# Windowed attention and a rational-function FFN: from the framework's schedule to an order made by a list scheduler in the kernel source

## The chip, the cores and the metric

The kernel runs on one core of one Trainium2 chip. The metric is the device time of one execution in microseconds; the lower the better. Before the change, three runs took 1013.21, 1014.49 and 1015.51 us, so the median is 1014.49.

## The reference

Attention with 8 batches, 8 heads, 576 positions and 64 features per head. Each position sees itself and the 63 positions before it. The 4608 rows of 512 features that come out go through a feed-forward layer whose activation is a quotient of two polynomials.

```python
scores = scale * np.matmul(q, k.transpose(0, 1, 3, 2))
mask = (rel >= 0) & (rel < window)            # window = 64
scores = np.where(mask, scores, -1000000000.0)
attn = np.exp(scores - np.max(scores, axis=-1, keepdims=True))
attn = attn / (np.sum(attn, axis=-1, keepdims=True) + 1e-09)
x = np.matmul(attn, v)                        # then 4608 x 512
h = x @ w_in                                  # w_in 512 x 2048
P = a[0] + a[1] * h + a[2] * h**2 + a[3] * h**3
Q = 1.0 + np.abs(b[0]) * np.abs(h) + np.abs(b[1]) * h**2
out = (P / (Q + 1e-6)) @ w_out                # w_out 2048 x 512
```

The weights arrive as 64-bit floating-point numbers and are decoded on the chip.

## The kernel before

**Tiling.** The 4608 tokens are 12 chunks of 384. A chunk has an attention part of four *units* (two heads each), and an FFN part of 16 *steps*, one for each 128 of the 2048 hidden features. There are 192 steps and 48 units. The order of the steps is: first half of chunk 0, first half of chunk 1, second half of chunk 1, second half of chunk 0, then chunks 2 to 11 whole. So the weights of the first eight steps are used twice before those of the second half are needed, at step 16.

**A weight block** (`decode`, L110, 32 of them: 16 of `w_in`, 16 of `w_out`): a load of 512 KB, an ACT operation (L124), one on POOL (L127), two on DVE (L128, L129), one on ACT (L132, the high part) and one on DVE (L133, the low part). High and low parts stay in SBUF for the whole run.

**A unit** (L153 to L249): loads of q, k and v; 12 rows of score matmuls on PE into `ps_s` (L200); for chunks 1 and 2 the mask is added by two further matmuls (L193), for the others by two operations on DVE (L211); a maximum (L214, or L207 with L208); six exponentials on ACT (L221, L218); sums and reciprocals (L223, L224); the normalisation (L225), which is on DVE for chunk 0 and on POOL for the rest; transposes on PE into the same single `ps_s` buffer (L232) and a copy of them on ACT (L234); value products on PE (L243); the result split in a high and a low part, `xh` on ACT (L248) and `xl` on DVE (L249).

**A step** has two products on PE with a gate between them. `ffn1` (L253): 12 matmuls into one of two `h` buffers (L258); then the gate, with five operations on ACT (L265 to L267, L273, L274), one on POOL (L270) and six on DVE (L268, L269, L275 to L278). DVE's last one writes `gl`, the low half of the gate; `gh` is the high half. L269 is the last one to read `h`. `ffn2` (L288): nine matmuls (L298) that add the step's share to three accumulators `o`. I write H(s) and O(s) for the two products of step s.

**Half results.** When the first half of chunk 0 ends, its three accumulators are copied to a constant SBUF tile `part` (L305), and added back on DVE (L310) at the end of the second half.

**What sets the order.** The program text issues loads, units, H(s) and O(s - 3) from a table `todo`, with blocks and units placed at fixed steps (L322 to L347). The tile framework then schedules the instructions again by its own timeline simulation (`schedule_with_timeline_sim=True`, L403), so the order on each engine isn't that of the text. Each engine works through its own queue in order, and so does the queue of DMAs on SP.

**Buffers** that matter here: three stages for loaded weights (`w_st`), two `w_c`, two v tiles, two sets of gate temporaries (`tmp`), four pairs `gh`, `gl` (`gp`), two `h`, one `ps_s`, one `ps_x`.

Of the kernel before, what the change touches and what calls it, by code (L numbers as in the profile page):

```python
# [22 lines left out]
W_AT = 0, 1, 2, 3  # L23
WLEAD = len(W_AT)
NEG = -1.0e30
PEM = 1, 2
QADD = 1.0 + 1e-6


@with_exitstack  # L30
def swa_rational_ffn(ctx: ExitStack, tc: tile.TileContext, qT, kT, v, w_in, w_out, a, b, out):
# [20 lines left out]
    gp = ctx.enter_context(tc.tile_pool(name="gp", bufs=LAG + 1))  # L52
# [57 lines left out]
    def decode(src, hi, lo):  # L110

        w = stage.tile([P, 512, 2], U32, name="w_st", bufs=3)
        if len(src.shape) == 3:
            nc.sync.dma_start(out=w.rearrange("p (c n) two -> p c (n two)", c=src.shape[1]), in_=src)
        else:
            nc.sync.dma_start(out=w.rearrange("p n two -> p (n two)"), in_=src)
        low, high = w[:, :, 0], w[:, :, 1]
        c = stage.tile([P, 512], U32, name="w_c")
        cf = c.bitcast(F32)

        highf = w.bitcast(F32)[:, :, 1]
        nc.scalar.activation(cf, highf, AF.Copy, scale=2.0 ** -111)  # L124


        nc.gpsimd.tensor_scalar(out=highf, in0=highf, scalar1=0.0, scalar2=None, op0=ALU.mult)  # L127
        nc.vector.scalar_tensor_tensor(out=c, in0=c, scalar=3, in1=high, op0=ALU.logical_shift_left, op1=ALU.bitwise_or)  # L128
        nc.vector.scalar_tensor_tensor(out=c, in0=low, scalar=29, in1=c, op0=ALU.logical_shift_right, op1=ALU.bitwise_or)  # L129
        if len(hi.shape) == 3:  # L130
            cf = cf.rearrange("p (c n) -> p c n", c=hi.shape[1])
        nc.scalar.activation(hi, cf, AF.Copy, scale=2.0 ** -8)  # L132
        nc.vector.scalar_tensor_tensor(out=lo, in0=cf, scalar=2.0 ** -8, in1=hi.bitcast(F32), op0=ALU.mult, op1=ALU.subtract)  # L133

    def load_w_in(i):
        sl = slice(i * P, (i + 1) * P)
        decode(w_in[i], wi_h[:, :, sl], wi_l[:, :, sl])

    def load_w_out(i):
        decode(w_out_v[:, i, :], wo_h[:, i, :], wo_l[:, i, :])  # L140
# [12 lines left out]
    def unit_load(c, hp):  # L153
        q = kv.tile([P, TC, WIN], F32, name="q")
        kt = kv.tile([P, TC + 1, WIN], F32, name="kt")
        vt = kv.tile([P, TC, P], F32, name="vt")
        kw, vw, first = [], [], None
        j = kb = vb = 0
        for bi, t0, n in segments(c):
            nc.sync.dma_start(out=q[:, j:j + n, :].rearrange("p t s -> p (t s)"),  # L160
                              in_=qT[bi, hp, :, t0 * WIN:(t0 + n) * WIN])
# [16 lines left out]
        m0 = None if first is None else MASKS[first]
        live[c, hp] = dict(q=q, kt=kt, vt=vt, kw=kw, vw=vw, m0=m0)
# [108 lines left out]
    def ffn2(s):  # L288
# [3 lines left out]
        if first:  # L292
            acc[c] = [ps_o.tile([P, DO], F32, name=f"o{t}") for t in range(NTS)]
# [115 lines left out]
```

## Time and profile before

| | |
|---|---|
| median of 3 runs | 1014.49 us (1013.21 to 1015.51) |
| span of the profiled execution | 1014.7 us |
| PE busy | 954.8 us (94%) |
| DVE busy | 825.9 us (81%) |
| ACT busy | 725.1 us (71%) |
| POOL busy | 324.9 us (32%) |
| mean granted clock of TensorE | 0.971 |
| read and written in HBM | 53.48 and 9.44 MB |

The profile lists the span, from the first to the last instruction; what may lie around it has no row. Durations below are of this one execution. Busy shares are means over the whole run, so the table alone doesn't say what bounds which stage. "Idle before" in a row is time in which the engine had nothing to do ahead of that group, with what ended it. Records of one engine overlap a little, since an instruction's end is pipelined with the start of the next: start to start is shorter than the duration shown.

### The profile page before, as it was taken

Reading aid. Unit: us, or ns where it says so; the run is one execution under the profiler, and the core shown is the slowest. Engines: PE = TensorE matmul, PEld = TensorE weight load, DVE = VectorE, ACT = ScalarE, POOL = GpSimd, SP = SyncE. Lnnn points to the kernel's source line nnn. Section 1 sums busy time; section 2 is a strip of 40 time slices with the busy share of each in tenths; the row PEclk is TensorE's granted clock in tenths of the full one; section 3 lists DMA queues with packets and bytes.
Section 4 is the critical chain, followed back from the end, with each engine's and each line's share of the span. In section 5 each row is a group of like instructions: output and inputs, shape, how many; then the busy total and the mean of one; then the engine's idle time right before and its main releaser. Section 6 shows DMA issues by size and latency. Waiting matters only on the chain.

```text
span 1014.7 us, 18277 instructions
## 1 busy us (share of the span) xinstructions
PE 954.8 (94%) x6640; PEld 844.8 (83%) x6640; DVE 825.9 (81%) x1539; ACT 725.1 (71%) x1735; POOL 324.9 (32%) x283
## 2 busy tenths in 40 slices
PE   3688578999999999999999999999999999999997
PEld 2576367989898888898888888888988988988996
DVE  7899788878888788788788787787787888787885
ACT  5777666667676777877777777777777777777664
POOL 4566544223332222223223223223223223222221
PEclk9679789999999999999999999999999999999999
DMA  7634630021211211210211211110121111100000
GB/s 239 221 110 138 207 98 16 1 77 29 90 31 31 83 42 34 88 37 29 76 46 31 67 58 34 64 61 29 61 61 31 62 63 35 64 17 1 32 1 31
DMA packets 37817, 64.09 MB, mean 63 GB/s; under 512 B 4448, under 2 KB 24928, under 8 KB 37728
## 3 DMA queue, kind: packets, MB, share of 16 engines
q1 hardware_dynamic: 37728, 62.93, 19.4%
q8 instruction: 52, 0.85, 0.4%
q14 instruction: 37, 0.30, 0.1%
HBM read 53.48 MB, written 9.44 MB: 62 GB/s over the span
## 4 chain that ended last, share of the span: by engine, by line
PE 84%; DVE 10%; ACT 3%; issue 2%; POOL 1%; DMA 1%; SPq 0%; POOLq 0%; DVEq 0%
PE h L258 38%; PE o L298 37%; PE ps_x L243 3%; PE ps_s L200 3%; PE ps_s L232 3%; DVE w_c L128 2%; POOL w_st L127 1%; DVE w_c L129 1%; DVE wo_l L133 1%; DVE num L277 1%; DVE u L276 1%; DVE wi_l L133 1%; DVE gh L275 1%; DMA w_st<-w_in 1%; ACT w_c L124 0%
## 5 line engine op out<-in xcount | busy, mean ns | idle before, releaser
L270 POOL TENSOR_TENSOR u<-u,ah 128x384 f32<-128x384 f32 x192 | 198.2, 1033 | 383.3 <-ACT u L267 343.7
L258 PE MATMUL h<-xl,wi_h 128*128 128x384 f32 x768 | 267.5, 348 | 20.3 <-DVE num L269 18.6
L258 PE MATMUL h<-xh,wi_h 128*128 128x384 f32 x768 | 262.7, 342 | 0.0
L258 PE MATMUL h<-xh,wi_l 128*128 128x384 f32 x768 | 262.5, 342 | 0.0
L298 PE MATMUL o<-wo_h,gl 128*128 128x512 f32 x576 | 233.5, 405 | 7.2 <-DVE gl L278 7.2
L298 PE MATMUL o<-wo_h,gh 128*128 128x512 f32 x576 | 228.3, 396 | 0.0
L298 PE MATMUL o<-wo_l,gh 128*128 128x512 f32 x576 | 227.0, 394 | 0.0
L268 DVE TENSOR_TENSOR num<-num,h 128x384 f32<-128x384 f32 x192 | 106.2, 554 | 111.9 <-ACT num L266 111.5
L265 ACT ACTIVATE ah<-h 128x384 f32<-128x384 f32 x192 | 94.5, 492 | 124.1 <-PE h L258 84.9
L258 PEld LDWEIGHTS h<-xl,wi_h 128*128 128x128 f32 x768 | 147.3, 192 | 27.8 <-DVE num L269 20.7
L258 PEld LDWEIGHTS h<-xh,wi_h 128*128 128x128 f32 x768 | 147.4, 192 | 4.8
L225 POOL TENSOR_TENSOR sm<-sm,rs 128x768 f32<-128x768 f32 x44 | 68.4, 1555 | 253.2 <-DVE rs L224 250.5
L258 PEld LDWEIGHTS h<-xh,wi_l 128*128 128x128 f32 x768 | 147.0, 191 | 0.6 <-issue 0.2
L275 DVE SCALAR_TENSOR_TENSOR gh<-num,a_sb,ah 128x384 fp32r<-128x384 f32 x192 | 119.3, 633 | 28.4 <-ACT ah L274 28.3
L298 PEld LDWEIGHTS o<-wo_h,gl 128*128 128x128 f32 x576 | 109.0, 189 | 33.7 <-DVE gl L278 8.8
L267 ACT ACTIVATE u<-ah,b_sb 128x384 f32<-128x384 f32 x192 | 135.6, 707 | 0.0
L221 ACT ACTIVATE sm<-sm,nmx 128x128 f32<-128x128 f32 x240 | 93.3, 390 | 57.4 <-DVE nmx L214 57.4
L298 PEld LDWEIGHTS o<-wo_h,gh 128*128 128x128 f32 x576 | 109.3, 190 | 25.2
L266 ACT ACTIVATE num<-h,a_sb 128x384 f32<-128x384 f32 x192 | 128.3, 668 | 0.0
L298 PEld LDWEIGHTS o<-wo_l,gh 128*128 128x128 f32 x576 | 109.2, 190 | 18.5
L269 DVE SCALAR_TENSOR_TENSOR num<-num,a_sb,h 128x384 f32<-128x384 f32 x192 | 117.7, 614 | 6.1
L277 DVE SCALAR_TENSOR_TENSOR num<-num,a_sb,u 128x384 f32<-128x384 f32 x192 | 116.7, 622 | 0.4
(52 smaller groups left out, 1139.2 us busy)
## 6 DMA issues: line engine op xcount, KB each, us to landing
out<-ob SPq DMA_DIRECT2D x33, 256.0 KB, 2.5
w_st<-w_in SPq DMA_DIRECT2D x16, 512.0 KB, 3.7
w_st<-w_out SPq DMA_DIRECT2D x16, 512.0 KB, 4.2
q<-qT SPq DMA_DIRECT2D x32, 192.0 KB, 3.2
vt<-v SPq DMA_DIRECT2D x16, 384.0 KB, 3.1
vt<-v SPq DMA_DIRECT2D x16, 320.0 KB, 3.0
kt<-kT SPq DMA_DIRECT2D x16, 224.0 KB, 3.6
kt<-kT SPq DMA_DIRECT2D x16, 192.0 KB, 3.4
```

Source lines behind the costliest of these rows:

```text
L221: nc.scalar.activation(sm[:, j, :], sm[:, j, :], AF.Exp, bias=nmx[:, j:j + 1], accum_out=sums[:, j:j + 1])
L225: (nc.vector if c < 1 else nc.gpsimd).tensor_tensor(out=sm, in0=sm, in1=rs.unsqueeze(2).broadcast_to([P, NR, P]), op=ALU.mult)
L258: nc.tensor.matmul(h, w[:, cc, i * P:(i + 1) * P], x[c, cc], start=n == 0, stop=n == 3 * NCC - 1)
L265: nc.scalar.activation(ah, h, AF.Abs)
L266: nc.scalar.activation(num, h, AF.Identity, scale=a_sb[:, 3:4], bias=a_sb[:, 2:3])
L267: nc.scalar.activation(u, ah, AF.Identity, scale=b_sb[:, 1:2], bias=b_sb[:, 0:1])
L268: nc.vector.tensor_tensor(out=num, in0=num, in1=h, op=ALU.mult)
L269: nc.vector.scalar_tensor_tensor(out=num, in0=num, scalar=a_sb[:, 1:2], in1=h, op0=ALU.add, op1=ALU.mult)
L270: nc.gpsimd.tensor_tensor(out=u, in0=u, in1=ah, op=ALU.mult)
L275: nc.vector.scalar_tensor_tensor(out=gh, in0=num, scalar=a_sb[:, 0:1], in1=ah, op0=ALU.add, op1=ALU.mult)
L277: nc.vector.scalar_tensor_tensor(out=num, in0=num, scalar=a_sb[:, 0:1], in1=u, op0=ALU.add, op1=ALU.subtract)
L298: nc.tensor.matmul(acc[c][t], g[:, ts], w[:, i, :], start=first and n == 0, stop=last and n == 2)
```

## The change

The program text no longer issues work as it goes. Each piece is first described as an `Op`: its engine, a cost in microseconds, a rank (about the step at which it is wanted), what it comes after, and the buffers that it takes. `Plan.order` then builds a schedule: on each engine it looks for the operations that could start first, and among those within 0.02 us of the earliest takes the one of the lowest rank. It counts a hand-over of 0.035 us between engines, the overlap at an operation's end (`TAIL`), buffers that come free, one DMA bus, and half as much again for a DVE operation that runs beside POOL. The instructions are emitted in the order of the planned starts, in a section in which the framework leaves the order alone.

```diff
+class Plan:
+    LATENCY = 0.035
+    TAIL = {"PE": 0.16, "DVE": 0.083, "ACT": 0.105, "POOL": 0.0}
...
+    def order(self):
...
+            for e in ENGINES:
+                able = []
+                for op in ready[e]:
+                    if any(not slots[s.pool] for s in op.takes):
+                        continue
+                    t = max([free[e], op.ready] + [min(slots[s.pool]) for s in op.takes])
+                    able.append((t, op))
...
+                t0 = min(t for t, _ in able)
+                t, op = min(((t, op) for t, op in able if t <= t0 + 0.02), key=lambda x: (x[1].rank, x[0]))
+                if best is None or t < best[0]:
+                    best = t, op
...
+            if op.shares and free["POOL"] > t:
+                cost += 0.5 * min(cost, free["POOL"] - t)
...
+        return sorted(self.ops, key=lambda o: o.start)
...
-    gp = ctx.enter_context(tc.tile_pool(name="gp", bufs=LAG + 1))
+    gp = ctx.enter_context(tc.tile_pool(name="gp", bufs=3))
...
+    plan = Plan({"w_st": 3, "w_c": 2, "qk": 2, "vt": 1, "sm": 2, "pT": 1, "ps_s": 1, "ps_x": 1, "h": 2, "tmp": 2, "gp": 3,
+                 "o0": 1, "o1": 1, "o2": 1, "spill": 1})
...
+        o = plan.add("SP", 2.3, rank - 2, load, uses=[st])
+        o = plan.add("ACT", 0.68, rank, scale, [o], [st, sc])
+        o = plan.add("POOL", 1.75, rank, sign, [o], [st])
+        o = plan.add("DVE", 0.685, rank, put_sign, [o], [st, sc], True)
+        o = plan.add("DVE", 0.685, rank, put_low, [o], [st, sc], True)
+        o = plan.add("ACT", 0.635, rank, high, [o], [sc])
+        return plan.add("DVE", 0.685, rank, rest, [o], [sc], True)
...
+            vt = u["vt"] = kv.tile([P, TC, P], F32, name="vt", bufs=1)
...
-        (nc.vector if c < 1 else nc.gpsimd).tensor_tensor(out=sm, in0=sm, in1=rs.unsqueeze(2).broadcast_to([P, NR, P]), op=ALU.mult)
+            nc.gpsimd.tensor_tensor(out=sm, in0=sm, in1=u["rs"].unsqueeze(2).broadcast_to([P, NR, P]), op=ALU.mult)
...
+        f = f1[s] = plan.add("PE", 2.245, s, products, x_ready[c] + [tile_in[i], f1.get(s - 1)], [sh])
...
+            o = plan.add("PE", 0.855, s + LAG + 0.5 + 0.01 * t, lambda t=t: products(t),
+                         [gate_done[s], tile_out[i], f2.get((s - 1, t)), f2.get((s, t - 1))], [sg, so[t]])
...
-            part[c] = const.tile([P, NTS, DO], F32, name="part")
-            for t in range(NTS):
-                nc.scalar.copy(out=part[c][:, t, :], in_=o[t])
+                ob = e["ob"] = stage.tile([P, DO], F32, name="spill", bufs=1)
...
+                part[c, t] = tc.dram_tile([P, DO], F32, name=f"part{c}_{t}")
+                nc.sync.dma_start(out=part[c, t], in_=e["ob"])
...
+        tile_in[i] = plan_decode(w_in[i], wi_h[:, :, sl], wi_l[:, :, sl], need[i] - 1.5)
+        tile_out[i] = plan_decode(w_out_v[:, i, :], wo_h[:, i, :], wo_l[:, i, :], need[i] + LAG - 1.5)
...
+    load_coefficients()
+    with tc.manual_schedule():
+        for op in plan.order():
+            op.emit()
```

Beside the order, five things change. There is one v tile in place of two. There are three `gh`, `gl` pairs in place of four. The half results of chunk 0 go through one SBUF buffer (`spill`) to a tile in DRAM and are fetched into weight stages before they are added. The normalisation of chunk 0 moves from DVE to POOL. The two loads of coefficients stand ahead of all others. The steps, the units, their chunks and the arithmetic stay.

Three places in the order. The first is DVE after the low half of gate 7. Before, a long run of decode operations stands here (`w_c`, `wi_l`, `wo_l` are the decode's):

```order
L133 SCALAR_TENSOR_TENSOR wo_l<-w_c,wo_h 128x512
L129 SCALAR_TENSOR_TENSOR w_c<-w_st,w_c 128x512
L133 SCALAR_TENSOR_TENSOR wi_l<-w_c,wi_h 128x4x128
L128 SCALAR_TENSOR_TENSOR w_c<-w_c,w_st 128x512
L129 SCALAR_TENSOR_TENSOR w_c<-w_st,w_c 128x512
L128 SCALAR_TENSOR_TENSOR w_c<-w_c,w_st 128x512
L133 SCALAR_TENSOR_TENSOR wo_l<-w_c,wo_h 128x512
L129 SCALAR_TENSOR_TENSOR w_c<-w_st,w_c 128x512
L249 TENSOR_TENSOR xl_915<-ps_x,xh_914 128x384
```

Now, behind the same gate, operations of the gates alternate with those of the decode (L241, L246 and L257 are now the decode's three, L452 to L482 the gate's six):

```order
L469 SCALAR_TENSOR_TENSOR gh<-num,a_sb,ah 128x384
L241 SCALAR_TENSOR_TENSOR w_c<-w_c,w_st 128x512
L473 SCALAR_TENSOR_TENSOR u<-u,gh 128x384
L246 SCALAR_TENSOR_TENSOR w_c<-w_st,w_c 128x512
L477 SCALAR_TENSOR_TENSOR num<-num,a_sb,u 128x384
L452 TENSOR_TENSOR num<-num,h 128x384
L482 TENSOR_TENSOR gl<-num,ah 128x384
L257 SCALAR_TENSOR_TENSOR wo_l<-w_c,wo_h 128x512
```

What moved: when the low half of gate 12 is done, 31 blocks were decoded before and 18 are now; for gate 20 it is 32 and 26, for gate 23 it is 32 and 31, for gate 24 both have all 32.

The second is PE around O(23), the output products of step 23. Before, they follow value products, and a masked score group comes after them:

```order
L243 MATMUL ps_x<-pT,vt 64x64 x12
L298 MATMUL o_1267<-wo_h,gl 128x512
L298 MATMUL o_1267<-wo_l,gh 128x512
L298 MATMUL o_1267<-wo_h,gh 128x512
L298 MATMUL o_1268<-wo_h,gl 128x512
L298 MATMUL o_1268<-wo_l,gh 128x512
L298 MATMUL o_1268<-wo_h,gh 128x512
L298 MATMUL o_1269<-wo_h,gl 128x512
L298 MATMUL o_1269<-wo_l,gh 128x512
L298 MATMUL o_1269<-wo_h,gh 128x512
L193 MATMUL ps_s<-mask,ident_r 128x384 x2
```

Now H(26) and a score group (L335) stand ahead of them, and H(27) behind:

```order
L437 MATMUL h<-xh_0_503,wi_l 128x384
L335 MATMUL ps_s<-kt,q 64x128 x12
L520 MATMUL o_1346<-wo_h,gl 128x512
L520 MATMUL o_1346<-wo_l,gh 128x512
L520 MATMUL o_1346<-wo_h,gh 128x512
L520 MATMUL o_1381<-wo_h,gl 128x512
L520 MATMUL o_1381<-wo_l,gh 128x512
L520 MATMUL o_1381<-wo_h,gh 128x512
L520 MATMUL o_1439<-wo_h,gl 128x512
L520 MATMUL o_1439<-wo_l,gh 128x512
L520 MATMUL o_1439<-wo_h,gh 128x512
L437 MATMUL h<-xl_0_263,wi_h 128x384
```

What moved: by O(23) the new order has issued the score groups of units 11 and 12 and the transposes of unit 11, which stood behind it; the number of H and O groups issued is the same.

The third is PE in a late unit. Before, value products and the next unit's scores are adjacent:

```order
L258 MATMUL h<-xh_2288,wi_l 128x384
L243 MATMUL ps_x<-pT,vt 64x64 x12
L200 MATMUL ps_s<-kt,q 64x128 x12
L298 MATMUL o_2696<-wo_h,gl 128x512
L298 MATMUL o_2696<-wo_l,gh 128x512
```

Now transposes (L378) and value products (L388) stand two output groups apart, and the score group stands two steps ahead of the transposes:

```order
L378 MATMUL ps_s<-ident,sm 128x128 x6
L520 MATMUL o_2674<-wo_h,gl 128x512
L520 MATMUL o_2674<-wo_l,gh 128x512
L520 MATMUL o_2674<-wo_h,gh 128x512
L520 MATMUL o_2681<-wo_h,gl 128x512
L520 MATMUL o_2681<-wo_l,gh 128x512
L520 MATMUL o_2681<-wo_h,gh 128x512
L388 MATMUL ps_x<-pT,vt 64x64 x12
L520 MATMUL o_2708<-wo_h,gl 128x512
```

What moved: the unit's three groups lie in three places. Between them H(s) and O(s - 3) now alternate one by one, where before two H often stood together, then two O. At the very end H(191) has O(188) to O(191) behind it, where it had O(189) to O(191).

More of the change, by code (lines that the diff above doesn't have):

```diff
@@ L30, in swa_rational_ffn @@
+ENGINES = "PE", "DVE", "ACT", "POOL", "SP"
 @with_exitstack
@@ L108, in swa_rational_ffn @@
     w_out_v = w_out.rearrange("(fc p) e -> p fc e", p=P)
[L110 to L140, printed above, removed]
+    C0 = 2
+    HA = 8
+    NU = HP
+    phases = [(c, 0, HA) for c in range(C0)] + [(c, HA, NF) for c in reversed(range(C0))] + [(c, 0, NF) for c in range(C0, NCH)]
+    steps = [(c, i) for c, i0, i1 in phases for i in range(i0, i1)]
+    total = len(steps)
+    begin, at = {}, {}
+    for s, (c, i) in enumerate(steps):
+        begin.setdefault(c, s)
+        at[c, i] = s
@@ L289, in ffn2, with plan_out @@
+    acc, part, sent = {}, {}, {}
+    so = {}
+    f2 = {}
+    def plan_out(s):
         c, i = steps[s]
@@ L291, in ffn2 @@
         last = s == total - 1 or steps[s + 1][0] != c
+        d, sg = gs.pop(s)
         if first:
-            acc[c] = [ps_o.tile([P, DO], F32, name=f"o{t}") for t in range(NTS)]
-        gh, gl = gs.pop((c, i))
-        for t in range(NTS):
-            ts = slice(t * P, (t + 1) * P)
-            for n, (g, w) in enumerate(((gl, wo_h), (gh, wo_l), (gh, wo_h))):
-                nc.tensor.matmul(acc[c][t], g[:, ts], w[:, i, :], start=first and n == 0, stop=last and n == 2)
-        if not last:
-            return
@@ L365, in swa_rational_ffn @@
[L365 to L375 removed]
+            for t in range(NTS):
+                so[t] = Slot(f"o{t}")
+        spill = c < C0 - 1 and i < HA
+        merge = c < C0 - 1 and i >= HA
@@ new lines, in products, with fetch @@
+        def products(t):
+            if first:
+                acc[t] = ps_o.tile([P, DO], F32, name=f"o{t}")
+            ts = slice(t * P, (t + 1) * P)
+            for n, (g, w) in enumerate(((d["gl"], wo_h), (d["gh"], wo_l), (d["gh"], wo_h))):
+                nc.tensor.matmul(acc[t], g[:, ts], w[:, i, :], start=first and n == 0, stop=last and n == 2)
+        def fetch(t, e):
+            ob = e["ob"] = stage.tile([P, DO], F32, name="ob", tag="w_st", bufs=3)
+            nc.sync.dma_start(out=ob, in_=part[c, t])
@@ new lines, in swa_rational_ffn @@
+    for c, i0, i1 in phases:
+        if c not in seen:
+            before = begin[c] - prev
+            for k in range(NU):
+                order.append((c, k, -12 + k if c == 0 else before + (prev // NU) * k - AHEAD))
+            seen.append(c)
+        prev = i1 - i0
+    last_step = {}
+    for s, (c, i) in enumerate(steps):
+        last_step[c] = s
+    holder = {}
+    n = 0
+    s = 0
+    for c, k, rank in order:
+        if c >= C0 and k == 0:
+            old = max(x for x in range(c) if slot_of[x] == slot_of[c])
+            while s <= last_step[old]:
+                plan_gate(s)
+                s += 1
+            free_x[c] = [f1[last_step[old]]]
+        plan_unit(c, k, rank)
@@ L378 @@
+    while s < total:
+        plan_gate(s)
+        s += 1
+    for s in range(total):
+        plan_out(s)
+    load_coefficients()
+    with tc.manual_schedule():
+        for op in plan.order():
+            op.emit()
 _OUTS = [((4608, 512), 'float32')]
```

489 lines of the change are left out of this document (305 added, 184 removed).

## The prediction

> **What bounds the kernel now.** I read the page's busy slices first, then the same question by stage in a table of windows, then the operations of DVE in the early stage.
>
> ```profile
> PE   3688578999999999999999999999999999999997
> DVE  7899788878888788788788787787787888787885
> ...
> 5.40:163.00 157.60, 107.37 (x799) 89.82 (x800) 142.26 (x232) 108.82 (x277) 85.48 (x52) 0.83 0.49 157
> ...
> 300.00:900.00 600.00, 600.00 (x4301) 535.46 (x4301) 485.56 (x939) 449.19 (x1091) 172.76 (x157) 1.00 0.16 51
> ```
>
> In the slices (25.4 us each) PE is full from the seventh on. In the windows (length, then busy PE, PEld, DVE, ACT, POOL) PE is busy 600 of 600 us late, but 107.37 of 157.60 early, where DVE is busy 142.26: idle for only 15.3 us. So there are two stages. Late, PE is the bound and nothing that another engine saves is worth anything. Early, DVE is, and the longest waits of PE are for it:
>
> ```profile
> PE h L258 <- DVE num L269: 18.6, 7, 5.9
> ```
>
> Now what DVE did in those 157.6 us (by line: busy us, mean ns, idle before):
>
> ```profile
> L129 DVE SCALAR_TENSOR_TENSOR w_c<-w_st,w_c 128x512 uint32<-128x512 uint32 x32 | 26.0, 814 | 0.2
> L128 DVE SCALAR_TENSOR_TENSOR w_c<-w_c,w_st 128x512 uint32<-128x512 uint32 x32 | 25.0, 781 | 6.8 <-POOL w_st L127 6.6
> L133 DVE SCALAR_TENSOR_TENSOR wo_l<-w_c,wo_h 128x512 fp32r<-128x512 f32 x16 | 13.3, 833 | 0.4 <-ACT wo_h L132 0.4
> L133 DVE SCALAR_TENSOR_TENSOR wi_l<-w_c,wi_h 128x512 fp32r<-128x512 f32 x16 | 12.7, 791 | 1.9 <-ACT wi_h L132 1.9
> L275 DVE SCALAR_TENSOR_TENSOR gh<-num,a_sb,ah 128x384 fp32r<-128x384 f32 x13 | 10.6, 812 | 3.0 <-ACT ah L274 3.0
> L277 DVE SCALAR_TENSOR_TENSOR num<-num,a_sb,u 128x384 f32<-128x384 f32 x13 | 9.8, 756 | 0.1
> L276 DVE SCALAR_TENSOR_TENSOR u<-u,gh 128x384 f32<-128x384 f32 x13 | 9.1, 702 | 0.2
> L269 DVE SCALAR_TENSOR_TENSOR num<-num,a_sb,h 128x384 f32<-128x384 f32 x14 | 8.4, 602 | 0.0
> L268 DVE TENSOR_TENSOR num<-num,h 128x384 f32<-128x384 f32 x14 | 7.5, 543 | 0.0
> L278 DVE TENSOR_TENSOR gl<-num,ah 128x384 fp32r<-128x384 f32 x13 | 7.1, 547 | 0.0
> L207 DVE TENSOR_REDUCE nmx<-ps_s 128x6 f32<-128x768 f32 x6 | 5.7, 946 | 0.0
> L249 DVE TENSOR_TENSOR xl<-ps_x,xh 128x384 fp32r<-128x384 f32 x8 | 4.4, 544 | 0.0
> L225 DVE TENSOR_TENSOR sm<-sm,rs 128x768 f32<-128x768 f32 x4 | 4.3, 1070 | 0.1
> L211 DVE SCALAR_TENSOR_TENSOR sm<-ps_s,mask 128x384 f32<-128x384 f32 x8 | 4.1, 548 | 0.7 <-PE ps_s L200 0.7
> L214 DVE TENSOR_REDUCE nmx<-sm 128x6 f32<-128x768 f32 x4 | 3.8, 947 | 0.0
> ```
>
> All 32 weight blocks are decoded here (77.0 us), but only 13 steps are gated: blocks that steps 16 to 23 need are decoded while PE starves for gates of steps 8 to 12. These rows sum to 151.8 us and the window has 142.26 busy, since records overlap: a factor of 0.937.
>
> **The change: the start.** The new order puts gates ahead of decodes that are not due. That removes no decode; all 32 are due by step 24. So I compare at one point, the output products of step 23:
>
> ```profile
> 212.70 1.02 DVE L278 TENSOR_TENSOR gl<-num,ah 128x384 fp32r<-128x384 f32 x2
> 215.76 0.51 PE L298 MATMUL o<-wo_h,gl 128*128 128x512 f32 x1
> ```
>
> Before, they begin at 215.76, and 1014.7 - 215.76 = 798.9 us follow. In the new order DVE has, up to the low half of gate 23: 31 decodes of 0.814 + 0.781 + 0.812 (mean of the two L133 rows) = 74.6; 24 times four gate operations of 2.82 together and 25 times two of 1.145, 96.2; eight maxima of 0.946, ten xl of 0.544, and the masked rows 4.1 and 3.8, 20.9. The four normalisations (4.3) are gone to POOL. Sum 191.7, times 0.937: 179.6 us. The window begins with DVE's first mask, at 5.4; the coefficient loads now go ahead of the first q and k:
>
> ```profile
> 4.60 0.71 SPq L89 DMA_DIRECT2D a_sb<-a  x1
> 5.35 0.53 SPq L90 DMA_DIRECT2D b_raw<-b  x1
> ```
>
> So 1.2 us more, 6.7. **Idle time** of DVE is not to be seen in advance. Lower end 8: the 15.3 without the 6.6 that waited for POOL's decode step, which an order could avoid. Upper end 30, twice today's. For more: chunk 0's four units pass one by one through the single `ps_s`, and each now waits for POOL. For less: decodes that are not urgent can fill. I take 16, close to the row. Gate 23 is then done at 6.7 + 179.6 + 16 = 202.3. The row ahead of it in DVE's order frees the `h` buffer for step 26, whose products and one score group stand ahead on PE: 2.5 us, O(23) at 204.8. Step 27 waits likewise, an estimated 1.2.
>
> On POOL a normalisation takes 1.56 us, where the row above has 1.07 on DVE:
>
> ```profile
> L225 POOL TENSOR_TENSOR sm<-sm,rs 128x768 f32<-128x768 f32 x44 | 68.4, 1555 | 253.2 <-DVE rs L224 250.5 <-ACT ah L273 2.7
> ```
>
> **The rest of the run.** Around O(23) PE is ahead by a transpose and two score groups, 0.57 + 0.82 + 1.27 (one with its mask, an estimate) = 2.7 us less to do. Then the unit's three groups stand apart, where value and score products were adjacent:
>
> ```profile
> 402.82 0.39 PE L298 MATMUL o<-wo_h,gh 128*128 128x512 f32 x1
> 403.06 0.82 PE L232 MATMUL ps_s<-ident,sm 128*128 128x128 f32 x6
> 403.63 0.42 PE L258 MATMUL h<-xl,wi_h 128*128 128x384 f32 x1
> 403.89 0.34 PE L258 MATMUL h<-xh,wi_h 128*128 128x384 f32 x1
> 407.78 0.34 PE L258 MATMUL h<-xh,wi_l 128*128 128x384 f32 x1
> 408.05 0.92 PE L243 MATMUL ps_x<-pT,vt 128*64 128x64 f32 x24
> 408.89 0.89 PE L200 MATMUL ps_s<-kt,q 64*64 64x128 f32 x24
> 409.71 0.51 PE L298 MATMUL o<-wo_h,gl 128*128 128x512 f32 x1
> 410.05 0.40 PE L298 MATMUL o<-wo_l,gh 128*128 128x512 f32 x1
> ```
>
> Start to start, a value group takes 0.84, a score group 0.82, transposes 0.57. Leaving a group costs 0.1 (0.34 to the second o matmul, 0.24 in the row of o's) and entering the value group 0.1. One more exit and at most one more entry per unit, 36 units: 0 to 7 us, I take 5. Three `gp` buffers for four cost nothing there: a gate is written after its step's h, and the product that frees its buffer follows that h at once.
>
> **The end.** Before, the last gate comes late and the clock falls:
>
> ```profile
> 1004.61 0.40 PE L298 MATMUL o<-wo_h,gh 128*128 128x512 f32 x1
> 1007.27 0.50 PE L298 MATMUL o<-wo_h,gl 128*128 128x512 f32 x1 [2.26 <-DVE gl L278]
> 1007.61 0.54 PE L298 MATMUL o<-wo_l,gh 128*128 128x512 f32 x1
> ```
>
> Now three output steps, not two, stand behind the last h, so nine matmuls at 0.23 or 2.07 of the 2.26 go, and of the slow matmuls behind an estimated 9 x (0.54 - 0.40) = 1.3: 3.4 us.
>
> **Half results in memory** cost three copies and three stores through one buffer, one after the other, before chunk 1 may use the third accumulator:
>
> ```profile
> L312 ACT COPY ob<-o x30: 569/579/622, 216.9 to 947.5; 128x512 f32<-128x512 f32 x30
> out<-ob SPq DMA_DIRECT2D x33, 256.0 KB, 2.5
> ```
>
> That is 3 x (0.58 + 2.5) = 9.2 us. PE's order puts three steps of h and parts of two output steps there, and DVE has decodes to do: 0. Uncovered it is some 5, within the idle range. The fetch rides on idle DMA. One value buffer makes each load wait for the previous unit; late units are four steps apart, 730.6 / 152 x 4 = 19 us by the row of ob (steps 23 to 175), and early that belongs to the idle term.
>
> **Sum:** 204.8 + 1.2 + 798.9 - 2.7 + 5 - 3.4 = 1003.8. The span of 1014.7 is 0.2 above the median of the runs, 1014.49; I forecast **1004 us**.
>
> A rule that speaks against the move to POOL: the Trainium skill, page "SBUF — State Buffer", section "SBUF: two separate sides", says that DVE and GpSimd lock a shared port pair and the loser blocks for the other's whole instruction. By it the four moved operations could cost DVE 6.2 us where it saves 4.3, and the sum would be 1004 to 1010. The trace agrees in part: early, gh, num and u with two SBUF inputs took 812, 756 and 702 ns, while num with h from PSUM (543, 602) is short; but gl, with two SBUF inputs, is short too (547).
>
> **The rivals.** (1) *DVE packs tightly:* idle 4 to 8, 10 less: 993. For it: the new order counts hand-overs; against: 15.3 us idle with the same chains today. (2) *The start is no faster:* idle 27, so 1015. The unit chains through one `ps_s`, one `vt` and POOL speak for it; PE then starts its first h no sooner than today. (3) *PE waits for the transposes late, slower than before:* between a score group and its transposes lie two steps, about 8.4 us (the row of ob spans 730.6 us and 152 steps, 4.81 a step, less a quarter of the unit's groups). The chain is two masks, a maximum, six exponentials and a normalisation:
>
> ```profile
> L221 ACT ACTIVATE sm<-sm,nmx 128x128 f32<-128x128 f32 x240 | 93.3, 390 | 57.4 <-DVE nmx L214 57.4
> ```
>
> 1.1 + 0.95 + 2.34 + 1.56 = 5.95, with some 2.4 left for queues on DVE (81% busy) and ACT (75%). Over that, each microsecond is paid in all 36 late units. It decides from 0.3 us a unit, where 11 us of gain are gone; at 0.7 the time is 1029. (4) *The order does not come out as written* is excluded: the rows shown ahead are the built program's.
>
> **How the numbers follow.** Forecast 0.50 (997 to 1010), tight packing 0.18, no gain 0.14, late waits 0.18. The range must leave out 2 in 10: 988 (tight, and no cost of the groups) to 1018 (no gain, or waits up to 0.4). A measurement of this kernel tells about 0.2% from no change. Faster by that (below 1012.5): forecast, tight packing and a little of no gain, 0.70; within: 0.12; slower: 0.18.
>
> **What would show it.** Right: O(23) begins at about 205, DVE idle about 16 before it, far more than 13 gates done by 163; from 210 on PE is full; time per four steps up by 0.14 us; the last wait of PE below 0.5. Wrong: PE idle before the transposes late (rival 3), a sum of DVE's rows up to gate 23 far from 180 (contention), or DVE idle above 25 (rival 2).

## The result, and the profile after

The changed kernel takes 1046.19 us (median of 4 runs, 1045.51 to 1047.38), the kernel before 1014.74 us (1013.21 to 1015.51, 4 runs) beside it. The ratio is 1.031, 95% interval 1.029 to 1.033: **slower by 3.1%**, where 1004 us and a gain were forecast.

PE's busy slices of the changed kernel (26 us each) and its windows (length, then busy PE, PEld, DVE, ACT, POOL, granted clock, DMA share, GB/s):

```profile
PE   4687996899999999999999999999999999999998
```

```profile
8.14:210.50 202.36, 156.42 (x1130) 129.72 (x1130) 183.80 (x302) 142.16 (x358) 105.76 (x69) 0.96 0.41 128
300.00:900.00 600.00, 580.45 (x4110) 502.99 (x4109) 517.99 (x892) 423.42 (x1025) 197.69 (x149) 1.00 0.15 49
```

PE still reads 9 in all late slices but the last, but a 9 covers everything from 90%: the window shows 580.45 of 600 us, where it was 600 of 600. The clock is no reason, 1.00 in both. So I cut at the same place as the prediction, the first output matmul of step 23, with gate 23 ahead of it:

```profile
209.94 0.54 DVE L482 TENSOR_TENSOR gl<-num,ah 128x384 fp32r<-128x384 f32 x1
...
214.87 0.51 PE L520 MATMUL o<-wo_h,gl 128*128 128x512 f32 x1
```

The start gains 0.9 us (214.87 for 215.76). From there to the end it takes 1044.5 - 214.87 = 829.6 us where it took 798.9: **the loss of 30.7 us is in the late stage.** The waits of PE from 220 us on, in the changed kernel (total, times, longest):

```profile
PE ps_x L388 <- ACT pT L382: 22.2, 35, 0.7
PE ps_s L378 <- POOL sm L373: 2.6, 4, 1.2
...
```

Once in each late unit, the value products (L388) wait 0.63 us for the copy `pT`. With two waits of 0.3 these are 25.4 us; the same view of the kernel before has one wait of 2.3. So the view accounts for 23.1 of the 30.7 us; experiment 6 shows where shorter waits hide from it. Now what got longer there. Groups by line from 220 to 940 us, first of the kernel before, then of the changed one (busy, mean ns, idle before):

```profile
L278 DVE TENSOR_TENSOR gl<-num,ah 128x384 fp32r<-128x384 f32 x150 | 80.9, 553 | 1.3
...
L270 POOL TENSOR_TENSOR u<-u,ah 128x384 f32<-128x384 f32 x150 | 152.9, 1021 | 281.0 <-ACT u L267 244.7 <-PE ps_s L200 36.3
L225 POOL TENSOR_TENSOR sm<-sm,rs 128x768 f32<-128x768 f32 x37 | 54.5, 1473 | 234.4 <-DVE rs L224 234.4
```

```profile
L482 DVE TENSOR_TENSOR gl<-num,ah 128x384 fp32r<-128x384 f32 x144 | 146.4, 1017 | 2.4
...
L459 POOL TENSOR_TENSOR u<-u,ah 128x384 f32<-128x384 f32 x143 | 178.2, 1246 | 334.0 <-ACT u L449 334.0
L373 POOL TENSOR_TENSOR sm<-sm,rs 128x768 f32<-128x768 f32 x35 | 57.6, 1646 | 153.9 <-DVE rs L369 148.5 <-ACT u L449 5.4
```

The same operations on the same data: `gl` takes 1017 ns for 553, POOL's `u` 1246 for 1021, the normalisation 1646 for 1473. One unit in order of time shows how (start, duration; its score group is the first row, and other rows between are left out):

```profile
391.42 0.89 PE L335 MATMUL ps_s<-kt,q 64*64 64x128 f32 x24
...
399.02 1.66 POOL L373 TENSOR_TENSOR sm<-sm,rs 128x768 f32<-128x768 f32 x1 [4.33 <-DVE rs L369]
...
399.39 1.71 DVE L482 TENSOR_TENSOR gl<-num,ah 128x384 fp32r<-128x384 f32 x1
...
400.64 1.33 POOL L459 TENSOR_TENSOR u<-u,ah 128x384 f32<-128x384 f32 x1
400.74 0.87 PE L378 MATMUL ps_s<-ident,sm 128*128 128x128 f32 x6
...
402.00 0.53 ACT L462 ACTIVATE ah<-u 128x384 f32<-128x384 f32 x1 [2.04 <-POOL u L459]
...
402.80 0.79 ACT L382 COPY pT<-ps_s 128x768 f32<-128x768 f32 x1
...
403.65 0.28 PE L388 MATMUL ps_x<-pT,vt 128*64 128x64 f32 x2 [0.65 <-ACT pT L382]
```

`gl` starts 0.37 us after POOL's normalisation and ends at 401.10, 0.42 behind the normalisation's end at 400.68: it did its work only then. This is no single case: from 300 to 900 us 89 of the 119 low halves in the trace begin beside a running POOL operation, and all 89 end 0.41 to 0.42 us behind it; in the kernel before none of 126 ran beside one. POOL's `u` starts at 400.64, while `gl` still runs, and takes 1.33. The logarithm (L462) waits for `u`, and the copy stands behind it and one more operation on ACT, although the transposes ended at 401.61. The Trainium skill, page "SBUF — State Buffer", section "Who interferes with whom", says that a DVE instruction with two SBUF inputs contends with a GpSimd one that reads SBUF, and that the order of issue decides who blocks. By that rule `gl` waits for all of the normalisation; these rows agree.

### The profile page after: what moved, and what is told of

It is laid out like the page before. It is cut to its first block, busy times and chain, and to the rows that moved or that the text cites. A ratio compares the mean times of both kernels' runs of the same rounds, so it can differ in the third digit from the quotient of the medians.

```text
span 1044.5 us, 18358 instructions
## 1 busy us (share of the span) xinstructions
PE 962.8 (92%) x6640; PEld 830.8 (80%) x6640; DVE 905.7 (87%) x1535; ACT 724.5 (69%) x1735; POOL 370.8 (36%) x287
## 4 chain that ended last, share of the span: by engine, by line
DVE 45%; PE 18%; ACT 14%; POOL 12%; issue 9%; DMA 1%; DVEq 0%; POOLq 0%; SPq 0%; ACTq 0%
PE h L437 8%; POOL u L459 8%; DVE gh L469 8%; DVE u L473 7%; PE o L520 6%; DVE num L477 5%; DVE gl L482 5%; DVE num L455 4%; POOL sm L373 4%; DVE sm L341 3%; DVE nmx L352 3%; ACT pT L382 3%; ACT ah L443 3%; DVE num L452 3%; ACT ah L465 3%
## 5 line engine op out<-in xcount | busy, mean ns | idle before, releaser
L459 POOL TENSOR_TENSOR u<-u,ah 128x384 f32<-128x384 f32 x192 | 233.4, 1216 | 438.9 <-ACT u L449 394.9
L437 PE MATMUL h<-xl,wi_h 128*128 128x384 f32 x768 | 261.1, 340 | 6.5 <-ACT wi_h L254 3.7
L437 PE MATMUL h<-xh,wi_h 128*128 128x384 f32 x768 | 259.3, 338 | 0.0
L462 ACT ACTIVATE ah<-u 128x384 f32<-128x384 f32 x192 | 101.0, 526 | 226.5 <-POOL u L459 226.5
L520 PE MATMUL o<-wo_h,gl 128*128 128x512 f32 x576 | 239.6, 416 | 15.3 <-ACT wo_h L254 11.2
L469 DVE SCALAR_TENSOR_TENSOR gh<-num,a_sb,ah 128x384 fp32r<-128x384 f32 x192 | 122.8, 640 | 84.1 <-ACT ah L465 74.5
L482 DVE TENSOR_TENSOR gl<-num,ah 128x384 fp32r<-128x384 f32 x192 | 186.4, 971 | 2.5
L373 POOL TENSOR_TENSOR sm<-sm,rs 128x768 f32<-128x768 f32 x48 | 78.7, 1640 | 188.3 <-DVE rs L369 169.3
L477 DVE SCALAR_TENSOR_TENSOR num<-num,a_sb,u 128x384 f32<-128x384 f32 x192 | 123.7, 645 | 1.9
L473 DVE SCALAR_TENSOR_TENSOR u<-u,gh 128x384 f32<-128x384 f32 x192 | 110.2, 575 | 14.6 <-DVE gh L469 0.5
```

The costliest lines, as they stand in the source:

```text
L373: nc.gpsimd.tensor_tensor(out=sm, in0=sm, in1=u["rs"].unsqueeze(2).broadcast_to([P, NR, P]), op=ALU.mult)
L437: nc.tensor.matmul(h, w[:, cc, i * P:(i + 1) * P], x[c, cc], start=n == 0, stop=n == 3 * NCC - 1)
L459: nc.gpsimd.tensor_tensor(out=d["u"], in0=d["u"], in1=d["ah"], op=ALU.mult)
L462: nc.scalar.activation(d["ah"], d["u"], AF.Ln, bias=QADD)
L469: nc.vector.scalar_tensor_tensor(out=d["gh"], in0=d["num"], scalar=a_sb[:, 0:1], in1=d["ah"], op0=ALU.add, op1=ALU.mult)
L473: nc.vector.scalar_tensor_tensor(out=d["u"], in0=d["u"], scalar=QADD, in1=d["gh"].bitcast(F32), op0=ALU.add, op1=ALU.mult)
```

## The experiments

All start from the changed kernel (1046 us). Ratios are to the kernel before in the same batch, with 95% intervals. Each tile name and line is as above.

**1. `gl` without its second SBUF input, from step 24 on.** The order on every engine stays. The kernel leaves the factor `ah` out of `gl`, so `gl` no longer reads that tile:

```diff
-            nc.vector.tensor_tensor(out=d["gl"], in0=d["num"], in1=d["ah"], op=ALU.mult)
+            nc.vector.tensor_tensor(out=d["gl"], in0=d["num"], in1=d["ah"], op=ALU.mult) if s < 24 else nc.vector.tensor_reduce(out=d["gl"], in_=d["num"].rearrange("p (n k) -> p n k", k=1), axis=AX.X, op=ALU.max)
```

> From step 24 on the low half gl is made by an operation of DVE of the same size with one SBUF input in place of two (it leaves out the factor ah). Order and dependencies on all engines stay. Theory C (DVE's gl and POOL's operations shut each other out of SBUF, and this makes POOL's u, then the logarithm, then the copy pT late): gl falls from 1017 ns to about 550, u on POOL from 1246 to 1020 to 1100, the normalisation from 1646 to 1480 to 1600, PE's wait for pT from 22.2 to 4 to 10 us, time 1026 to 1034. Rival (the long gl is only DVE's slack and the copy is late by ACT's order alone): gl falls but the wait stays at 18 to 22 and the time at 1042 to 1046.

Measured: 1019.56 us, ratio 1.0044 (1.0028 to 1.0060). The row of `gl` from 300 to 900 us, a `u` right behind a normalisation, and PE's waits from 220 on:

```profile
L482 DVE TENSOR_REDUCE gl<-num 128x384 fp32r<-128x384 f32 x123 | 67.4, 548 | 2.1
```

```profile
395.40 1.00 POOL L459 TENSOR_TENSOR u<-u,ah 128x384 f32<-128x384 f32 x1
```

```profile
PE ps_s L378 <- POOL sm L373: 1.1, 2, 0.6
PE ps_x L388 <- ACT pT L382: 0.6, 2, 0.3
PE o L520 <- DVE gl L482: 0.3, 1, 0.3
```

26.6 us of the loss are gone, and all waits but 2.0. The meeting of `gl` with POOL caused the late loss. It gave more than I expected (1026 to 1034), and not quite in the way that I expected. By their means POOL's two operations hardly got shorter (1197 ns for 1260 and 1653 for 1653 in this window), so other DVE operations still hold them up. But the `u` right behind the normalisation, for which the logarithm and so the copy wait, took 1.00 us for 1.32 (medians of 35 late units): here theory C holds, and the mean hides it. And `gl` also stands between mask and maximum of a unit, where it is shorter too: the normalisation ends 7.96 us behind the score group for 8.38.

**2 and 3. The place of the wait.** In the late units the value products one output group later on PE; and, apart from that, the copy ahead of the logarithm on ACT. Both move planned operations before they are emitted:

```diff
+        if op.emit.__name__ == "values" and op.rank > 25:
+            n = ops.index(op)
+            m = next(k for k in range(n + 1, len(ops)) if ops[k].engine == "PE")
+            if ops[m].emit.__name__ == "<lambda>":
+                ops.insert(m + 1, op)
+                del ops[n]
```

```diff
+        if op.emit.__name__ == "copy_pT" and op.rank > 25:
+            while True:
+                n = ops.index(op)
+                m = next(k for k in range(n - 1, -1, -1) if ops[k].engine == "ACT")
+                if ops[m].emit.__name__ not in ("logarithm", "absolute") or op.start - ops[m].start > 2.5:
+                    break
+                ops.insert(n, ops.pop(m))
```

> In the late units the value products stand one output group (0.69 us) later on PE; nothing else moves. Theory A (the late loss is PE's wait for the copy pT, which is due only 0.2 to 0.4 us before the value products): the wait of 22.2 us falls below 3, and the time from 1046 to 1022 to 1028. Rival B (the late loss is PE's own time, in groups that stand apart, and the wait only fills it): 1040 or more. Rival D (whatever is late for the value products is late for the next thing too): the wait turns up at the output products or at H, and the time stays above 1035.

> In the late units ACT copies the transposes (pT) ahead of the logarithm and the absolute value that stood before it; PE, DVE and POOL keep their order. Theory A with ACT's order as its place (the copy is ready at the end of the transposes and waits behind a logarithm that waits for POOL): the copy starts 0.7 to 1.1 us sooner, PE's wait of 22.2 us falls below 3, time 1022 to 1028. Rival D (the gate is delayed in exchange: the logarithm starts 0.4 to 0.8 us later): a wait of PE at the output products for gl, time above 1035. Rival B (PE's own time): 1040 or more.

Measured: 1058.26 us, ratio 1.0420 (1.0398 to 1.0443), and 1044.98 us, ratio 1.0286 (1.0268 to 1.0304). PE's longest wait late, first with the value products later, then with the copy first:

```profile
PE ps_s L378 <- POOL sm L373: 33.8, 35, 1.2
```

```profile
PE ps_s L378 <- POOL sm L373: 23.6, 36, 1.1
```

The wait for `pT` is gone, as theory A had it, and the time isn't: it stands at the transposes now, 0.97 and 0.66 us a unit. Theory A falls. Of rival D the time came, but not the place: it named the output products or H. Rival B, PE's own time in groups that stand apart, is out by experiment 1, where they stand apart just so. Why the transposes are late shows in the copy-first kernel, DVE ahead of a unit's exponentials, and POOL in the same stretch:

```profile
390.53 0.55 DVE L341 SCALAR_TENSOR_TENSOR sm<-ps_s,mask 128x384 f32<-128x384 f32 x1
391.00 1.33 DVE L477 SCALAR_TENSOR_TENSOR num<-num,a_sb,u 128x384 f32<-128x384 f32 x1
392.26 0.55 DVE L341 SCALAR_TENSOR_TENSOR sm<-ps_s,mask 128x384 f32<-128x384 f32 x1
392.73 0.54 DVE L482 TENSOR_TENSOR gl<-num,ah 128x384 fp32r<-128x384 f32 x1
393.19 0.94 DVE L352 TENSOR_REDUCE nmx<-sm 128x6 f32<-128x768 f32 x1
```

```profile
390.91 1.01 POOL L459 TENSOR_TENSOR u<-u,ah 128x384 f32<-128x384 f32 x1 [2.73 <-ACT u L449]
```

The second mask stands behind the remainder (L477) of a gate, and that meets POOL's `u`, which began 0.09 us sooner: 1.33 us instead of 0.6. In the changed kernel it was the other way round, by 0.05 us:

```profile
393.20 0.61 DVE L477 SCALAR_TENSOR_TENSOR num<-num,a_sb,u 128x384 f32<-128x384 f32 x1
393.73 0.55 DVE L341 SCALAR_TENSOR_TENSOR sm<-ps_s,mask 128x384 f32<-128x384 f32 x1
394.20 0.91 DVE L482 TENSOR_TENSOR gl<-num,ah 128x384 fp32r<-128x384 f32 x1
395.04 0.94 DVE L352 TENSOR_REDUCE nmx<-sm 128x6 f32<-128x768 f32 x1
```

```profile
393.25 1.45 POOL L459 TENSOR_TENSOR u<-u,ah 128x384 f32<-128x384 f32 x1 [2.87 <-ACT u L449]
```

There POOL was the one held up, and `gl` met its end. Over 300 to 900 us the remainder's mean goes from 604 to 787 and 786 ns in the two experiments. So an edit that saved 0.6 us on PE turned this meeting round, by 0.14 us, and lost it again.

**4. Both groups later on PE** (transposes and value products by one output group each, all else as it was).

> In the late units the transposes and the value products each stand one output group (0.69 us) later on PE; all other engines keep their order. Theory E (a chain that is up to 0.7 us too long for the PE work beside it): waits of PE late from 25 to below 8 us, time 1022 to 1030. Rival I (moving the unit's groups only shifts when POOL's and DVE's operations meet, so that a wait comes back elsewhere): waits above 15, time above 1035.

Measured: 1057.07 us, ratio 1.0426 (1.0410 to 1.0442). PE's waits late:

```profile
PE ps_x L388 <- ACT pT L382: 21.2, 33, 0.7
PE ps_s L378 <- POOL sm L373: 10.7, 35, 0.9
```

Rival I. The transposes got 0.69 us more room, but the normalisation now ends 9.44 us behind the score group for 8.38 (medians of 35 late units), since the remainder meets POOL's `u` as in experiment 2; its mean is 788 ns here too. The value products still wait for the copy behind the logarithm.

**5. The unit first on DVE.** In 35 late units both masks and the maximum one after the other, the remainder and `gl` behind them:

```diff
+        if op.rank > 25 and names[n - 4:n + 1] == ["<lambda>", "remainder", "<lambda>", "g_low", "maxima"]:
+            for x in dve[n - 1], dve[n - 3]:
+                ops.remove(x)
+                ops.insert(ops.index(op) + 1, x)
```

> In 35 late units DVE does both masks and the maximum one after the other; the remainder and the low half gl of an older gate, which stood between them, follow. All other engines keep their order. Theory E (the chain from the score group through masks, maximum, exponentials and normalisation to the transposes is longer than the PE work beside it, because gate operations stand in it that wait for POOL): the chain is 1.4 to 1.9 us shorter, PE's waits of 25 us at value products and transposes fall below 5, time 1019 to 1026. Rival F (the copy pT is late by the logarithm behind POOL's u, whatever the chain before it does): the wait for pT stays above 15, time above 1038.

Measured: 1042.83 us, ratio 1.0280 (1.0265 to 1.0296). PE's longest wait late:

```profile
PE ps_x L388 <- ACT pT L382: 21.5, 35, 0.6
```

Alone it does almost nothing: rival F, the copy behind the logarithm, is still in its place. The chain before it got only 0.15 us shorter, too (8.23 for 8.38): the maximum ends 1.23 us sooner, but from there to the reciprocal it takes 1.08 longer.

**6. Edits 3 and 5 together.** If a unit has two chains that each fill the PE work beside them, both have to be cut.

> Both late edits together on the order of the change: masks and maximum one after the other on DVE, and the copy pT ahead of the logarithm on ACT. Theory J (two chains of a unit, score group to transposes and transposes to value products, each fill the PE work beside them; cutting one leaves the other): where each alone left 22 to 24 us of waits, both together leave below 3 us, time 1018 to 1025. Rival I (each edit only shifts the meetings of POOL and DVE, and so would the two): waits above 15, time above 1035.

Measured: 1029.96 us, ratio 1.0159 (1.0142 to 1.0176). PE's waits late:

```profile
PE ps_s L378 <- POOL sm L373: 3.1, 5, 1.1
PE o L520 <- DVE gl L482: 0.3, 1, 0.3
```

Theory J in the main: where each alone left 22 to 24 us, both leave 3.4 (below 3 was expected). The time is 5 us above what I expected. The late stage takes 1026.9 - 215.38 = 811.5 us, where experiment 1 has 1019.1 - 216.15 = 803.0. Of these 8.5 us the view of waits accounts for 1.4. The rest are waits that it doesn't count, because most of each lies inside the record of the matmul before, whose end is modelled. PE's entry into the transposes, here and in the kernel of experiment 12, where PE is full:

```profile
396.82 0.34 PE L437 MATMUL h<-xh,wi_l 128*128 128x384 f32 x1
397.27 0.87 PE L378 MATMUL ps_s<-ident,sm 128*128 128x128 f32 x6
```

```profile
396.03 0.34 PE L437 MATMUL h<-xh,wi_l 128*128 128x384 f32 x1
396.20 0.82 PE L378 MATMUL ps_s<-ident,sm 128*128 128x128 f32 x6
```

Start to start it is 0.45 us for 0.17, and neither row is marked with a wait. Against experiment 1 such steps sum to the 8.5 us: into the transposes 0.52 for 0.22 on average (+10.9 in 36 units), between the transposes themselves +2.0, into the value products 0.32 for 0.44 (-4.4). So the first chain is still about 0.3 us too long here. Both chains, by the medians of 35 late units from 230 to 970 us (experiment 12's kernel is the last one below):

| kernel | end of score group to end of normalisation | end of transposes to value products |
|---|---|---|
| the change | 8.38 us | 2.03 us |
| 1, `gl` with one input | 7.96 | 1.43 |
| 3, copy first | 9.09 | 1.32 |
| 5, unit first | 8.23 | 2.01 |
| 6, both | 8.57 | 1.32 |
| 12, PE full | 7.94 | 1.32 |

With PE full, the transposes begin 8.36 us behind the score group and the value products 1.32 behind the transposes. A kernel is slow where one of its two figures doesn't fit into that, with some 0.05 us for the hand-over to the transposes.

**7. The other parts of the change undone:** two v tiles, four gate pairs, chunk 0's normalisation on DVE.

```diff
-            vt = u["vt"] = kv.tile([P, TC, P], F32, name="vt", bufs=1)
+            vt = u["vt"] = kv.tile([P, TC, P], F32, name="vt", bufs=2)
...
-    gp = ctx.enter_context(tc.tile_pool(name="gp", bufs=3))
+    gp = ctx.enter_context(tc.tile_pool(name="gp", bufs=4))
...
-            nc.gpsimd.tensor_tensor(out=sm, in0=sm, in1=u["rs"].unsqueeze(2).broadcast_to([P, NR, P]), op=ALU.mult)
+            (nc.vector if c < 1 else nc.gpsimd).tensor_tensor(out=sm, in0=sm, in1=u["rs"].unsqueeze(2).broadcast_to([P, NR, P]), op=ALU.mult)
```

> The order of the change with three of its other parts undone: two v tiles, four gate pairs, and chunk 0's normalisation on DVE in place of POOL. My theory: the late stage doesn't depend on these; at the start the four operations save some contention and cost DVE 4.3 us: time 1043 to 1047. Rival (the narrower buffers cost): 1035 or less, with fewer waits of PE late.

Measured: 1047.68 us, ratio 1.0309 (1.0290 to 1.0328), 0.7 us above my range and as slow as the change within the noise. With this order, whose late stage waits for the chains, they cost nothing that shows; whether they would cost something with PE full was not tried, nor were the half results in memory apart.

**8 and 9. The start.** Up to gate 23 DVE's decode rows in the changed kernel read

```profile
L241 DVE SCALAR_TENSOR_TENSOR w_c<-w_c,w_st 128x512 uint32<-128x512 uint32 x31 | 27.9, 904 | 0.3
L246 DVE SCALAR_TENSOR_TENSOR w_c<-w_st,w_c 128x512 uint32<-128x512 uint32 x31 | 25.8, 834 | 0.2
```

for 781 and 814 ns in the prediction's rows of before. So the decode's operation on POOL went to ACT, first at the same place of the same order, then with a new order from the scheduler (this operation as one of ACT, a hand-over of 0.08 us) and edit 3 together with a wider form of edit 5 (every gate operation between the masks goes behind the maximum). The decode takes the sign from a product with zero, and on ACT that product came out without a sign, so these kernels leave out the signs of the weights.

```diff
-            nc.gpsimd.tensor_scalar(out=highf, in0=highf, scalar1=0.0, scalar2=None, op0=ALU.mult)
+            nc.scalar.activation(highf, highf, AF.Copy, scale=0.0)
```

> The decode's operation on POOL (1.74 us, 32 times) is done by ACT (about 0.65 us) at the same place of the order; the rest stays. Theory G (at the start DVE is blocked by POOL: its rows up to gate 23 are 27 us longer than their medians): DVE's decode rows fall from 904 and 834 to below 800 ns, gate 23 is done at 196 to 204 in place of 210.5, time 1032 to 1040; the late stage stays at 829. Rival H (ACT, busy 144 of 206 us there, becomes the bound with 21 us more, or the single ps_s chain is): gate 23 after 207, time 1043 to 1048.

> The scheduler is given the decode's operation as one of ACT (0.65 us) and a hand-over of 0.08 us in place of 0.035, which makes a new order; then the late units get both masks and the maximum together on DVE, and the copy pT ahead of the logarithm. If theories E and G both hold: gate 23 done at 190 to 200, waits of PE late below 5 us, time 990 to 1005, faster than the kernel before. If only E: 1012 to 1022. If only G: 1020 to 1032.

Measured: the first 1047.28 us, ratio 1.0328 (1.0313 to 1.0344); the second **1001.08 us**, ratio 0.9868 (0.9852 to 0.9885). In the first, up to its gate 23:

```profile
8.14:209.30 201.16, 157.77 (x1134) 130.27 (x1133) 178.29 (x302) 159.86 (x390) 48.72 (x37) 0.96 0.41 130
```

DVE is busy 5.5 us less, but idle 22.9 us for 18.6: of what POOL no longer blocks, DVE waits for ACT in part (its waits for `ah` and the high parts of `w_in` rise from 2.2 to 6.6 us). The two decode rows fall to 819 and 825 ns, not below 800. Theory G falls as I put it, and rival H's time and gate (209.3) came, for this order. In the second, gate 23 is done at 195.5, and PE's waits late are 1.1 us.

**10. The new order without the move to ACT,** to tell the two apart.

> As the combination, but the decode's operation stays on POOL: a new order with a hand-over of 0.08 us, and the two late edits. Theory G' (the start is long because POOL's decode operation blocks DVE and waits for it, and taking it off POOL gave the combination its 15 us): gate 23 at 207 to 213, time 1015 to 1024. Rival (the new order alone gave them): gate 23 below 201, time 1000 to 1008.

Measured: 1021.18 us, ratio 1.0069 (1.0054 to 1.0084); gate 23 done at 210.9. Both lie in the ranges of theory G'. A new order with the operation left on POOL gains nothing at the start, and the move in the old order next to nothing; an order made for the operation on ACT gains 15 us. The two new orders differ, since the scheduler made each for its own place of the operation, so that blocking is the whole reason isn't shown. It also shows that the late loss can be taken away with POOL's work as it was; the late stage is 1019.4 - 214.84 = 804.6 us.

**11 and 12. The signs back.** First a tile of negative zeros as the operation's bias; it doesn't give the sign back, so this kernel leaves it out too. Then another decode: ACT makes the sign and multiplies it by -2, and DVE combines it with the shifted high word, bit by bit:

```diff
-            nc.scalar.activation(c.bitcast(F32), d["w"].bitcast(F32)[:, :, 1], AF.Copy, scale=2.0 ** -111)
+            nc.scalar.activation(c.bitcast(F32), d["w"].bitcast(F32)[:, :, 1], AF.Sign)
...
+            nc.scalar.activation(c, c, AF.Copy, scale=-2.0)
...
-            nc.vector.scalar_tensor_tensor(out=c, in0=c, scalar=3, in1=d["w"][:, :, 1], op0=ALU.logical_shift_left,
-                                           op1=ALU.bitwise_or)
+            nc.vector.scalar_tensor_tensor(out=c, in0=d["w"][:, :, 1], scalar=3, in1=c, op0=ALU.logical_shift_left,
+                                           op1=ALU.bitwise_xor)
```

(the factor of 1/256 behind it goes).

> The combination with the decode's operation on ACT, which now adds a tile of negative zeros so that the sign of the weights is kept. Expected as that combination: 999 to 1004, gate 23 done at 195 to 197, no waits of PE late. Rival (the operation with a tile for its bias is longer on ACT, by 0.1 us 32 times, at the stage where ACT is busy 170 of 202 us): 1004 to 1010.

> The combination (decode off POOL, new order with a hand-over of 0.08 us, the two late edits) with a decode that keeps the signs: ACT makes the sign and multiplies it by -2, DVE shifts the high word and combines the two bit by bit; as many operations on ACT and DVE as in the combination, none on POOL. Expected from theories G and J: gate 23 done at 194 to 199, no waits of PE late above 2 us, 998 to 1005, that is 1.0 to 1.5% below the kernel before. Rival (ACT's sign function or the changed operands are slower, or the order comes out otherwise): 1006 to 1016.

Measured: 1001.22 us, ratio 0.9875 (0.9859 to 0.9890), and **1001.52 us, ratio 0.9881 (0.9865 to 0.9898)**. The last computes all that the kernel before does, signs included, is 1.2% faster than it, and 4.3% below the changed kernel. Its window up to gate 23, the late window, its first output matmul of step 23, and one late group from 300 to 900 us:

```profile
8.14:193.10 184.96, 150.38 (x1107) 127.43 (x1108) 174.55 (x301) 156.77 (x387) 48.28 (x36) 0.96 0.45 140
300.00:900.00 600.00, 600.00 (x4280) 527.14 (x4279) 538.77 (x931) 440.24 (x1078) 190.86 (x156) 1.00 0.16 50
```

```profile
197.04 0.50 PE L520 MATMUL o<-wo_h,gl 128*128 128x512 f32 x1
```

```profile
L477 DVE SCALAR_TENSOR_TENSOR num<-num,a_sb,u 128x384 f32<-128x384 f32 x124 | 110.4, 890 | 3.3
L482 DVE TENSOR_TENSOR gl<-num,ah 128x384 fp32r<-128x384 f32 x125 | 94.5, 756 | 2.1
```

The means of remainder and `gl` add up to 1646 ns, for 1652 in the changed kernel in the same window (604 and 1048): they are blocked as much, and PE is full all the same. So blocking as such costs nothing late; it costs where it falls into a unit's chain from scores to value products. At the start DVE, up to gate 23, is busy 9.2 us less than in the changed kernel (174.6 for 183.8) and idle 8.2 less (10.4 for 18.6).

## Why the prediction was wrong, point by point

**The late stage** (the term of 798.9 us, kept from before) is where it failed. The prediction kept PE full there, and gave rival 3, waits for the transposes, 0.18. Its own sum for that chain was 5.95 us, "with some 2.4 left for queues". In the unit shown above the score group ends at 392.31 and the normalisation at 400.68: 8.37 us, so the 8.4 of room were used up to the last tenth. What the sum lacked are 0.43 us that the first mask stands behind a gate operation, 1.37 for the remainder and `gl` between masks and maximum, both on DVE, and about 0.7 for sums, reciprocal and hand-overs ahead of the normalisation. The kernel before had a warning, in the unit whose score group (408.89, 0.89 us) the prediction shows:

```profile
417.29 1.47 POOL L225 TENSOR_TENSOR sm<-sm,rs 128x768 f32<-128x768 f32 x1 [6.40 <-DVE rs L224]
422.28 0.82 PE L232 MATMUL ps_s<-ident,sm 128*128 128x128 f32 x6
```

From the end of the score group to that of the normalisation it took 8.98 us there, more than the 8.4 that the new order leaves; it cost nothing because the transposes came 12.5 us behind the score group. The rival had the right kind and sign. Its place was off: the wait shows at the value products first, behind ACT's logarithm, a second chain that the text did not price at all. That its size a unit came close (0.63 us in the view of waits, about 0.85 start to start against the kernel of experiment 12; the text named 0.7 as the case of 1029 us) is partly luck, since it stands at another place. That both chains are tight is shown by experiments 1, 2, 3, 5 and 6.

**The shared ports.** The prediction weighed the rule of the Trainium skill (page "SBUF — State Buffer", section "SBUF: two separate sides") for the four moved normalisations alone (6.2 us), and said that the trace agrees in part, since `gl` was short. That reading hid the loss. Late, `gl` was short in the kernel before (553 ns) because its order kept it apart from POOL. Early, in the window that the prediction read (547 ns), seven of the 13 ran beside POOL and still were short, and one of the POOL operations, a normalisation at 92.33 us, took 3.82 us for the 1.47 of the row above: there POOL was the one held up. So neither row shows `gl` to be exempt, and in the changed kernel 127 of 192 took over 0.7 us. The scheduler has the same gap: its cost for `gl` is 0.555 us and, alone of the gate's operations with two SBUF inputs on DVE, it isn't marked as sharing with POOL; POOL's `u` is planned at 1.035.

**The start.** Gate 23 was to be done at 202.3 and was at 210.5. The three terms: first mask at 8.14 for 6.7 (+1.4), DVE's work 183.8 for 179.6 (+4.2), idle 18.6 for 16 (+2.6). The first two were mis-sized, the third lies within its bounds of 8 to 30. The added work is of the size that the prediction had named for contention over the moved normalisations (up to 6.2), but it hardly comes from them: with them back on DVE, in experiment 7, DVE's work is 186.6 us, and 182.8 without their own 3.8. Then O(23) came 4.4 us behind gate 23 for 2.5: PE had six matmuls of O(22) still to do ahead of H(26) and the score group. Sum 10.1 us, nearly the whole gain of 10.5. The time at the start is that of rival 2, but not its cause, which was an idle time of 27.

**What held.** At 163 us 17 gates were done for 13, more but not far more. The tail: from the start of the last h matmul to that of the last output matmul 8.81 us (1031.55 to 1040.36), for 10.09 (1000.42 to 1010.51), with nine matmuls of 0.23 more in it: 3.4 saved, as forecast. The three `gp` buffers cost nothing that shows in this order: experiment 7. The groups that stand apart (+5) and the work that PE is ahead (-2.7) can't be told apart; in the last kernel, whose PE is full, the late stage is 997.5 - 197.04 = 800.5, 5.0 above 798.9 - 3.4, but with an order of its own. Two more things were inexact. PE is full from the eighth slice on, not from the seventh, which reads 8. And the sum set a span against the median of times, where in the profiled run of the changed kernel the time is 2.0 us above the span (1046.5 and 1044.5).

## What to carry to other kernels

Before a list schedule is trusted, compare an operation's mean duration by stage: where the same shape takes 553 ns in one order and 1017 in another, its cost depends on what runs beside it, and a plan with a fixed cost packs chains into room that isn't there. A chain's length is better read in the trace, from its first row to its last, than added up from the durations of its members, since the operations that stand between them are in it too. A chain that fits by a few tenths of a microsecond per round should be read as not fitting, and the wait should be traced to the chain, since an edit at the place where it shows can move it to the next tight chain. When two chains are equally tight, a null result for each edit alone says nothing against either. And a short wait can be missing from a view of waits: in experiment 6 PE lost about 0.3 us a unit that only the starts of its matmuls show.

## What was not expected of the hardware

- In the late units, who of DVE and POOL waited turned on less than 0.15 us: the remainder took 0.61 us when it began 0.05 us ahead of POOL's `u`, and 1.33 when it began 0.09 us behind. Moving a group on PE was enough to turn it. The recorded starts alone don't decide it everywhere: in the kernel before, the `gl` at 92.59 us took 0.54 us although a normalisation had begun 0.26 us ahead of it, and the normalisation waited. An older operation of DVE with two SBUF inputs, `gh`, was running then; that it kept POOL out is likely, but not shown.
- The blocked operation does its own work after the other's end, nearly whole: `gl` ended 0.41 to 0.42 us behind the POOL operation in 89 of 89 cases, and takes 0.55 alone. An operation of the same size with one SBUF input took 548 ns at the same places.
- On ACT, a negative number times zero came out without its sign, also with negative zeros added: by their distance from the reference, those kernels gave the result for weights that are all positive.
